# Output by pairs of token blocks on the upper and lower 64 lanes, and combine weights split on ScalarE and VectorE

## The chip, the core and the metric

One Trainium2 chip, one of its cores. The metric is the device time of one execution of the program, in microseconds (us). Before the change three runs took 404.69, 405.67 and 407.14 us, a median of 405.67. Engines are named as the profile names them: PE (TensorE matmul) and PEld (its weight loads), DVE (VectorE), ACT (ScalarE), POOL (GpSimd), SP (SyncE, which issues every DMA here).

## What is computed

Decayed causal attention over 8 batches, 8 heads and 576 tokens, whose output, as x of 4608 tokens by 512 columns, goes through a soft mixture of 8 experts with 4 slots each (32 slots):

```python
scores = where(causal, -1e9, q @ k.T / 8 + cum[:, None] - cum[None, :])
x = softmax(scores) @ v                      # 4608 tokens x 512
logits = x @ phi                             # 4608 x 32
d = softmax(logits, over tokens)             # dispatch
slot_out[e] = relu((d.T @ x)[e] @ w1[e]) @ w2[e]
c = softmax(logits, over slots)              # combine weights
out = c @ slot_out                           # 4608 x 512
```

All inputs and the output are float32. The last product, c times slot_out, is what the change is about: 4608 tokens by 32 slots by 512 columns, and 9.44 MB to be written to memory.

## The kernel before

The order of all instructions of an engine is the order in which the code writes them; nothing is rescheduled. Attention runs as a pipeline over 32 pairs of heads (the loop over `g`, from line 681). Meanwhile 23 of the 64 weight tiles of the experts (512 KB each, called quarters, 128 lanes by 1024 floats) are loaded into `w` tiles that stay in place; another 18 go into buffers that attention gives up at its end (`wstream`, line 124), and the last 23 are loaded into the first 23 tiles again, each as soon as the matmuls that read the old quarter are done. All these loads stand in SP's queue, in the order in which the experts use them.

After attention comes a tail. Slot inputs are summed up (`dispatch`, line 444), normalised, and then `STEPS` (line 35) lists, expert by expert, when its first matmul (`mlp1`, line 867) and the two halves of its second (`mlp2`, line 899) stand in PE's order. Experts 4 to 7 have their second matmul cut by output columns: the left 256 columns (half 0) come first, in the loop; the right 256 (half 1) come in the code behind the loop, whose eight weight quarters are the last eight to arrive.

Combine weights: `ctok` holds c by tokens. `split(b)` (line 655) takes batches b and b+4 and writes a rounded copy `hi` and the remainder `lo` to `cw`, both on POOL; `cols` (line 662) turns them on PE and copies them to `cT` on ACT. So `cT` has 128 lanes: lanes 0 to 63 are hi and lo of the 32 slots of batches 0 to 3, lanes 64 to 127 those of batches 4 to 7, and its 2304 columns are 18 blocks of 128 tokens. `split(0)` and `split(1)` stand at the last pair of heads (line 789), `split(2)` in the tail (836), `split(3)` at line 937, and `cols(3)` on line 939, behind the second matmul of expert 0.

Output: `gathered(n)` (line 965) adds half n of the columns of slot_out up in `so`, `slots(n)` (969) copies it to all lanes by a matmul, and `halve(h, n)` (972) splits it into a rounded part and a remainder, for the lower 64 lanes (h = 0) or the upper (h = 1); the other 64 lanes of these four `SO` tiles were filled with zeros on POOL (952). `blocks(n0, n1, c)` (981) makes token blocks n0 to n1 of 36: two matmuls of all 128 rows each, rounded part and remainder, into one PSUM bank, a copy to a stage tile (ACT and DVE in turn), and one DMA for the group. There are four banks for this and six stage tiles of 1024 columns. A block of one column half is 128 KB in rows of 1 KB; a whole one is 256 KB in rows of 2 KB. The first 20 blocks (`FIRST`) are made by halves, and the left halves of 15 of them stand between the last `mlp2` matmuls, three blocks to each weight quarter from the second of expert 5 on; the other 16 are made whole.

Of the kernel before, what the change touches and what calls it, by code (L numbers as in the profile page):

```python
# [16 lines left out]
NE, SPE, DM, DF = 8, 4, 512, 1024  # L17
NS = NE * SPE
P = 128
NPAIR = H // 2  # L20
NG = B * NPAIR
NBLK = 5
# [7 lines left out]
NQ = 8 * NE  # L30
QW = 1024
DEFER = 4
FIRST = 20

STEPS = (
    (0, 0), (1, 0), (2, 0), (3, 0), (0, 4), (0, 6), (1, 4), (1, 6), (4, 0), (5, 0), (2, 4), (2, 6), (3, 4), (3, 6),
# [34 lines left out]
def attn_softmoe(ctx: ExitStack, tc: tile.TileContext, qk, v, f, phi, w1, w2, cst, out):  # L71
# [89 lines left out]
    def turn():  # L161
        ring.append(ring.pop(0))
        return ring[-1]
# [488 lines left out]

    CW = {}

    def split(b):

        CW[b] = tp.tile([P, NBLK, 2, 2, NS], F32R, name=f"cw{b}", tag="cw", bufs=2)
        hi, lo = (CW[b][:, :, :, r].rearrange("p t h s -> p h t s") for r in range(2))
        nc.gpsimd.tensor_copy(hi, ctok[:, b::4])
        nc.gpsimd.tensor_tensor(lo, ctok[:, b::4], hi.bitcast(F32), op=ALU.subtract)  # L660

    def cols(b, bank):

# [17 lines left out]
    for g in range(1, NG):  # L681
# [104 lines left out]
        norm(h0)  # L786
        if g == 31:
            wstream(PTS[:, 0:QW])
            split(0)
            split(1)  # L790
        s3(h1)
        if w == 0:
            logits(b, *range(NPAIR))
# [10 lines left out]
    b = B - 1  # L804
    ring += [ps_s.tile([P, 512], F32, name=f"more{n}", tag="s") for n in range(2)]
    norm(NH - 1)
    dispatch(b - 1, 0, 1, 2)
    xt(NG - 1, (0, 4), nc.scalar.copy)
    xt(NG - 1, (2, 3), nc.vector.tensor_copy)
# [23 lines left out]
    nc.vector.tensor_reduce(mb[:, 2:3], EX[:, 0:192], axis=AX.X, op=ALU.add)  # L833
    total(b)
    nc.vector.tensor_scalar_mul(fin[:, 0:2], ones, lrun)
    split(2)
    dispatch(b, *range(NBLK))
    wstream(X[2], X[3])
    next(c2)
# [79 lines left out]
    for e, k in STEPS[:-4]:  # L919
        if k == 0:  # L920
            mlp1(e, 0, 1, 2, 3)
            relu(e)
        else:
            mlp2(e, k // 2 - 2)
        n = used + (2 if k else 4)
        wstream(*quarter[used : min(n, NRES)])
        used = n
        if (e, k) in ((2, 0), (4, 0), (6, 0), (5, 4)):
            own({2: 0, 4: 2, 6: 4, 5: 6}[e])
        if (e, k) == (1, 0):  # L930
            weigh(b)
            tokens(b, 0)
            combine(b, 0)
        if (e, k) == (3, 0):
            combine(b, 1)
            combine(b, 2)
            split(3)
        if (e, k) == (0, 6):
            for _ in cols(3, turn):
                pass  # L940
        if (e, k) == (1, 6):
            blank_h(4)
            blank_h(5)
        if (e, k) == (5, 0):
            late.close()
            sp = ctx.enter_context(tc.tile_pool(name="sp", bufs=1))
            so = sp.tile([P, DM], F32, name="so")

            SO = [[sp.tile([P, DM], F32R, name=f"SO{h}{r}") for r in range(2)] for h in range(2)]
            for h in range(2):  # L950
                for r in range(2):
                    nc.gpsimd.memset(SO[h][r][64 * (1 - h) : 64 * (1 - h) + 64].bitcast(F32), 0.0)
        if (e, k) == (3, 6):
            nc.scalar.copy(so, pv[0])
            blank_h(6)
            blank_h(7)

    half = [slice(256 * n, 256 * n + 256) for n in range(2)]
    pr = [t[:, 0:256] for t in bank]
    outv = out.rearrange("(n p) c -> p n c", p=P)  # L960
    NT = B * S // P
    stage = [t.rearrange("p a b -> p (a b)") for t in RAW] + p2 + p0
    copies = [nc.scalar.copy, nc.vector.tensor_copy]

# [4 lines left out]
    def slots(n):  # L969
        nc.tensor.matmul(pr[n], srep, so[:, half[n]], start=True, stop=True)  # L970

    def halve(h, *ns):
        rows = slice(64 * h, 64 * h + 64)
        for n in ns:
            c = half[n]
            nc.scalar.copy(SO[h][0][rows, c], pr[n][rows])
            nc.vector.tensor_tensor(SO[h][1][rows, c], pr[n][rows], SO[h][0][rows, c].bitcast(F32), op=ALU.subtract)

    state = [0, 0, 0]

    def blocks(n0, n1, c=slice(0, DM)):

        w = c.stop - c.start
        if state[1] + w * (n1 - n0) > QW:
            state[0:2] = state[0] + 1, 0
        o = stage[state[0] % len(stage)][:, state[1] : state[1] + w * (n1 - n0)]
        state[1] += w * (n1 - n0)
        for n in range(n0, n1):
            h, m = divmod(n, NT // 2)
            pm = turn()[:, 0:w]  # L990
            for r in range(2):
                nc.tensor.matmul(pm, cT[:, 128 * m : 128 * m + 128], SO[h][r][:, c], start=(r == 0), stop=(r == 1))  # L992
            copies[state[2] % 2](o[:, w * (n - n0) : w * (n - n0 + 1)], pm)
            state[2] += 1
        nc.sync.dma_start(outv[:, n0:n1, c], o.rearrange("p (n c) -> p n c", c=w))

    gathered(0)
    mlp2(4, 1, 0)
    slots(0)
    mlp2(4, 1, 1)  # L1000
    halve(0, 0)
    mlp2(5, 1, 0)
    n = 0
    for e, k in ((5, 1), (6, 0), (6, 1), (7, 0), (7, 1)):
        blocks(n, n + 2, half[0])
        mlp2(e, 1, k)
        blocks(n + 2, n + 3, half[0])
        n += 3
        if n == 9:
            halve(1, 0)  # L1010
    gathered(1)
    blocks(n, n + 2, half[0])
    slots(1)
    blocks(n + 2, n + 3, half[0])
    halve(0, 1)
    blocks(n + 3, FIRST, half[0])
    for n in range(0, FIRST, 2):
        blocks(n, n + 2, half[1])
        if n == 4:
            halve(1, 1)  # L1020
    for n in range(FIRST, NT, 2):
        blocks(n, n + 2)


# [39 lines left out]
```

## Time and profile before

| | |
|---|---|
| median of three runs | 405.67 us |
| the profiled execution: its own time | 407.26 us |
| the span of that profile | 405.5 us |
| PE busy in the span | 385.3 us (95%) |
| DVE, ACT, POOL busy | 281.7, 259.2, 257.6 us |
| attention's last matmuls with values end at | 331.8 us |
| last weight load is issued at | 366.6 us |
| first output DMA is issued at | 374.83 us |
| bytes moved by DMA | 93.72 MB |

The page cuts the span into 40 slices of some 10 us, with a digit for each engine's busy share; below them stand the clock granted to TensorE, the busy share of the 16 DMA engines and the GB/s that they moved. A row of windows gives for one stretch the busy time of each engine, with the number of instructions, then the granted clock, the DMA share and GB/s. The chain of waits is the work that ended last, followed back from the end: start, length, engine, tile, line. A group row gives a line's instructions of one shape: count, busy time and mean of one in ns, and behind the second bar the idle time before them. PE's single matmul records overlap one another, so what a matmul costs in a row of them is read from the chain, not from their mean.

### The profile page before, as it was taken

To read this page: it belongs to the slowest core of one execution; us is meant where nothing else is said; L and a number is where in the kernel's file an instruction comes from. 1 tells how busy PE (TensorE), PEld (TensorE's weight loads), DVE (VectorE), ACT (ScalarE), POOL (GpSimd) and SP (SyncE) were. 2 spreads that over 40 slices of the span, in tenths; PEclk is the share of its full clock that TensorE was granted. 3 is DMA by queue.
4 is the path that set the end of the run, shared out by engine and by line. 5 is a ranking of instruction groups with operands and counts; after the bars stand their busy time and mean duration, and the time that the engine had idled before them with its cause. 6 is when DMAs were issued, how large, how long until landed. Compare 5 with 4: busy or idle time off the path is not lost.

```text
span 405.5 us, 15191 instructions
## 1 busy us (share of the span) xinstructions
PE 385.3 (95%) x5871; PEld 339.3 (84%) x5871; DVE 281.7 (69%) x1127; ACT 259.2 (64%) x660; POOL 257.6 (64%) x351
## 2 busy tenths in 40 slices
PE   7888999999999999999999999999999999899990
PEld 6678999999999999998999999999999885345780
DVE  7784787878787977796879787878787533312571
ACT  8847776767786777686767786778685443100561
POOL 4694788777777777787778777877787742120000
PEclk9996999999999999999999999999999999999997
DMA  6773566677867787768767767777765699999698
GB/s 207 183 183 108 150 174 181 204 205 210 254 192 221 207 238 211 203 191 254 200 197 210 221 205 206 205 207 206 203 172 152 227 360 375 381 408 391 239 368 335
DMA packets 35192, 93.72 MB, mean 231 GB/s; under 512 B 4282, under 2 KB 10096, under 8 KB 35120
## 3 DMA queue, kind: packets, MB, share of 16 engines
q1 hardware_dynamic: 35120, 92.75, 74.0%
q8 instruction: 46, 0.75, 0.8%
q14 instruction: 26, 0.21, 0.1%
HBM read 63.93 MB, written 9.73 MB: 182 GB/s over the span
## 4 chain that ended last, share of the span: by engine, by line
PE 81%; DMA 4%; DVE 3%; ACT 3%; issue 1%; POOL 0%; SPq 0%; DVEq 0%; ACTq 0%
PE pv L309 24%; PE ring L274 13%; PE ring L275 11%; PE s L224 11%; PE pv L336 4%; DMA RAW<-in_qk 3%; PE lg L372 2%; PE pv L911 2%; PE ds L453 2%; PE ring L874 2%; PE pv L874 2%; PE more L992 2%; DVE s L237 1%; DMA out<-RAW 1%; PE ring L911 1%; PE ring L992 1%
## 5 line engine op out<-in xcount | busy, mean ns | idle before, releaser
L281 ACT ACTIVATE PTS<-ring 128x320 f32<-128x320 f32 (+2 forms) x256 | 119.7, 513 | 64.3 <-PE ring L275 36.7
L237 DVE CUSTOM_DVE_ANT_0 s<-s,mask 128x320 f32<-128x320 f32 (+4 forms) x320 | 137.7, 449 | 10.4 <-PE s L224 5.9
L274 PE MATMUL ring<-YA,WA 67*128 67x320 f32 (+9 forms) x384 | 123.3, 334 | 2.7 <-ACT PTS L281 1.7
L275 PE MATMUL ring<-YB,WB 128*128 128x320 f32 (+4 forms) x384 | 111.7, 299 | 0.0
L309 PE MATMUL pv<-V,PTS 128*64 128x65 f32 x3200 | 105.0, 224 | 0.6 <-ACT mr L256 0.6
L309 PEld LDWEIGHTS pv<-V,PTS 128*64 128x64 f32 x3200 | 100.3, 138 | 3.2 <-issue 1.2
L224 PE MATMUL s<-WA,YA 66*128 66x288 f32 (+9 forms) x384 | 98.9, 314 | 1.6 <-ACT YA L182 0.8
L203 POOL TENSOR_TENSOR WB<-RAW,WB 64x576 fp32r<-64x576 f32 x64 | 90.3, 1411 | 11.7 <-DMA WB<-WA 4.9
L208 POOL TENSOR_TENSOR YB<-RAW,YA 64x576 fp32r<-64x576 f32 x64 | 89.3, 1413 | 2.4
L274 PEld LDWEIGHTS ring<-YA,WA 67*128 67x128 f32 (+3 forms) x384 | 70.6, 185 | 9.0 <-issue 2.1
L275 PEld LDWEIGHTS ring<-YB,WB 128*128 128x128 f32 (+1 forms) x384 | 70.8, 184 | 0.0
L224 PEld LDWEIGHTS s<-WA,YA 66*128 66x128 f32 (+1 forms) x384 | 63.6, 192 | 7.3 <-ACT YA L182 1.1
L289 POOL TENSOR_SCALAR_AFFINE_SELECT PTS<-PTS 128x384 f32<-128x384 f32 x64 | 33.3, 521 | 32.0 <-ACT PTS L281 27.8
L292 POOL TENSOR_SCALAR_AFFINE_SELECT PTS<-PTS 128x128 f32<-128x128 f32 (+1 forms) x128 | 31.3, 265 | 34.8 <-ACT PTS L281 32.1
L237 DVE DVE_READ_ACCUMULATOR2_ANT MT<- 128x1 f32 x372 | 52.7, 142 | 0.0
L177 ACT CAST WA<-RAW 64x576 fp32r<-64x576 f32 x64 | 40.0, 669 | 14.2 <-DMA RAW<-in_qk 13.2
L336 PE MATMUL pv<-cs,X 128*128 128x128 f32 x155 | 42.9, 278 | 1.0 <-DVE X L329 0.8
L182 ACT CAST YA<-RAW 64x576 fp32r<-64x576 f32 x64 | 40.0, 670 | 0.4
L237 DVE CUSTOM_DVE_ANT_0 s<-s,mask,MT 128x288 f32<-128x288 f32 x62 | 32.6, 526 | 9.8 <-PE s L224 0.9
L324 DVE TENSOR_SCALAR rl<-pv 128x5 f32<-128x5 f32 x64 | 10.5, 164 | 34.7 <-PE pv L309 33.8
L329 DVE TENSOR_TENSOR X<-pv,rl 128x320 f32<-128x320 f32 (+1 forms) x65 | 31.5, 486 | 2.4 <-DMA YA<-mr 0.3
L360 ACT COPY XT<-pv 128x128 f32<-128x128 f32 (+1 forms) x124 | 28.7, 292 | 0.0
(202 smaller groups left out, 355.1 us busy)
## 6 DMA issues: line engine op xcount, KB each, us to landing
w<-in_w SPq DMA_DIRECT2D x46, 512.0 KB
RAW<-in_qk SPq DMA_DIRECT2D x31, 576.0 KB
V<-in_v SPq DMA_DIRECT2D x32, 325.0 KB
WB<-WA SPq DMA_DIRECT2D x31, 288.0 KB
YB<-YA SPq DMA_DIRECT2D x31, 288.0 KB
p<-in_w SPq DMA_DIRECT2D x7, 512.0 KB
out<-RAW SPq DMA_DIRECT2D x5, 512.0 KB
out<-RAW SPq DMA_DIRECT2D x9, 256.0 KB
```

Of the source, the lines that this page charges most:

```text
L177: nc.scalar.copy(WA[g % 3][0:64, S * h : S * h + S], RAW[g % 3][64:128, h])
L182: nc.scalar.copy(YA[g % 3][0:64, h, 64:640], RAW[g % 3][0:64, h])
L203: nc.gpsimd.tensor_tensor(t[0:64], RAW[g % 3][64:128, h], t[64:128].bitcast(F32), op=ALU.subtract)
L208: nc.gpsimd.tensor_tensor(YB[g % 2][64:128, h], RAW[g % 3][0:64, h], YA[g % 3][0:64, h, 64:640].bitcast(F32), op=ALU.subtract)
L224: nc.tensor.matmul(t[:, o : o + w], ya[0:m, h, 128 * blk : 128 * blk + 128], wa[0:m, j0 : j0 + w], start=True, stop=True)
L237: nc.vector.tensor_tensor_reduce(out=t[:, o : o + w], in0=t[:, o : o + w], in1=mask[:, m0 : m0 + w], scale=1.0, scalar=top if n == 3 else ...
L274: nc.tensor.matmul(o, wa[0:m, j0 : j0 + n], ya[0:m, h, 64 + i0 : 64 + i0 + w], start=True, stop=False)
L275: nc.tensor.matmul(o, wb[:, j0 : j0 + n], yb[:, h, i0 : i0 + w], start=False, stop=True)
L281: nc.scalar.activation(PT[i % 2][:, SEG_O[bank] : SEG_O[bank] + at], t[:, 0:at], AF.Exp, scale=0.125)
L289: nc.gpsimd.affine_select(d3, d3, pattern=[[0, 3], [1, 128]], compare_op=ALU.is_ge, fill=0.0, base=0, channel_multiplier=-1)
L309: nc.tensor.matmul(o[64 * u : 64 * u + 64, t, :], PT[i % 2][:, at : at + 64], V[:, g % 2, c, 65 * h : 65 * h + 65], start=(c == 0), stop=( ...
L336: nc.tensor.transpose(pm[:, 0:128], x[:, t, 128 * (p % 2) : 128 * (p % 2) + 128], ident)
```

## The change

- `split` makes `hi` on ACT and `lo` on DVE; nothing of it is left on POOL. For batches 0 and 1, `hi` stands where the whole split stood and `lo` behind the last normalisation of attention, on DVE.
- `cols(3)` moves two steps on, behind the second matmul of expert 1.
- `SO` is two tiles of 128 full lanes (rounded part, remainder), without zeros; `halve(n)` fills all lanes at once. The four memsets on POOL go.
- `blocks` goes by pairs: for m of 18, block m (batches 0 to 3) on lanes 0 to 63 and block m + 18 (batches 4 to 7) on lanes 64 to 127: four matmuls of 64 rows, the lower and the upper in turn, into two banks. ACT copies the lower block, DVE the upper. A single pair goes out in one DMA, two pairs in one DMA for each side.
- `FIRST` is 8 pairs, so 16 blocks are made by halves and 20 whole. No pair stands between the matmuls of one expert any more: two pairs behind expert 5, two behind expert 6, the rest behind expert 7.
- PSUM banks: two more for the output behind expert 5, two more behind the second `halve`.

```diff
-FIRST = 20
+FIRST = 8
...
-    def split(b):
+    def split(b, *parts):
...
-        nc.gpsimd.tensor_copy(hi, ctok[:, b::4])
-        nc.gpsimd.tensor_tensor(lo, ctok[:, b::4], hi.bitcast(F32), op=ALU.subtract)
+        if 0 in parts:
+            nc.scalar.copy(hi, ctok[:, b::4])
+        if 1 in parts:
+            nc.vector.tensor_tensor(lo, ctok[:, b::4], hi.bitcast(F32), op=ALU.subtract)
...
-            split(0)
-            split(1)
+            split(0, 0)
+            split(1, 0)
...
     norm(NH - 1)
+    split(0, 1)
+    split(1, 1)
...
-        if (e, k) == (0, 6):
+        if (e, k) == (1, 6):
             for _ in cols(3, turn):
...
+    def halve(n):
+        nc.scalar.copy(SO[0][:, half[n]], pr[n])
+        nc.vector.tensor_tensor(SO[1][:, half[n]], pr[n], SO[0][:, half[n]].bitcast(F32), op=ALU.subtract)
...
+    def blocks(m0, m1, c=slice(0, DM)):
...
+        for m in range(m0, m1):
+            pm = [turn()[:, 0:w] for _ in range(2)]
             for r in range(2):
-                nc.tensor.matmul(pm, cT[:, 128 * m : 128 * m + 128], SO[h][r][:, c], start=(r == 0), stop=(r == 1))
+                for h in range(2):
+                    rows = slice(64 * h, 64 * h + 64)
+                    nc.tensor.matmul(pm[h], cT[rows, 128 * m : 128 * m + 128], SO[r][rows, c], start=(r == 0), stop=(r == 1))
+            for h in range(2):
+                copies[h](o[:, h, m - m0], pm[h])
...
-    mlp2(5, 1, 0)
-    n = 0
-    for e, k in ((5, 1), (6, 0), (6, 1), (7, 0), (7, 1)):
-        blocks(n, n + 2, half[0])
-        mlp2(e, 1, k)
-        blocks(n + 2, n + 3, half[0])
-        n += 3
-        if n == 9:
-            halve(1, 0)
+    halve(0)
+    mlp2(5, 1)
+    ring += [bank[0], po[0]]
+    blocks(0, 1, half[0])
+    blocks(1, 2, half[0])
+    mlp2(6, 1)
+    blocks(2, 3, half[0])
+    blocks(3, 4, half[0])
+    mlp2(7, 1)
     gathered(1)
+    blocks(4, 6, half[0])
     slots(1)
+    blocks(6, FIRST, half[0])
+    halve(1)
+    ring += [bank[1], po[1]]
+    for m in range(0, FIRST, 2):
+        blocks(m, m + 2, half[1])
+    for m in range(FIRST, NT // 2):
+        blocks(m, m + 1)
```

Where PE turns the combine weights of batches 3 and 7 (lines 668 and 671, tiles `lg` and `ring` from `cw`): before, it comes between the first two experts' second matmuls (line 911, into `pv`).

```order
L911 MATMUL pv_148<-w_135,X_99 32x512 x2
L668 MATMUL lg_5604<-cs,cw_5905 128x128 x2
L668 MATMUL ring_150<-cs,cw_5905 128x128 x2
L668 MATMUL ring_150<-cs,cw_5905 128x64
L911 MATMUL pv_148<-w_136,X_100 32x512 x2
```

After, on PE at the same place, the second matmul of expert 1 (line 916) comes first.

```order
L916 MATMUL pv_148<-w_136,X_100 32x512 x2
L916 MATMUL pv_148<-w_137,X_100 32x512 x2
L916 MATMUL pv_148<-w_138,X_100 32x512 x2
L916 MATMUL pv_148<-RAW_97,X_100 32x512 x2
L671 MATMUL lg_5604<-cs,cw_5905 128x128 x2
```

So four rows of 512-column matmuls now stand ahead of the turning.

Where PE begins the output, before: the two weight quarters of expert 5 in half 1 (`w_133` and `w_134`, line 911) with the first two blocks between them (line 992).

```order
L911 MATMUL pv_148<-w_133,X_100 32x256 x4
L992 MATMUL ring_150<-SO_5984,cT 128x256
L992 MATMUL ring_150<-SO_5985,cT 128x256
L992 MATMUL more_5686<-SO_5984,cT 128x256
L992 MATMUL more_5686<-SO_5985,cT 128x256
L911 MATMUL pv_148<-w_134,X_100 32x256 x4
```

After, on PE at the same place (line 993 is the output matmul, 916 the expert's):

```order
L916 MATMUL pv_148<-w_133,X_100 32x256 x4
L916 MATMUL pv_148<-w_134,X_100 32x256 x4
L993 MATMUL ring_150<-SO_5984,cT 128x256
L993 MATMUL more_5684<-SO_5984,cT 128x256
L993 MATMUL ring_150<-SO_5985,cT 128x256
L993 MATMUL more_5684<-SO_5985,cT 128x256
```

Two quarters now stand together, and the two banks of a pair take turns.

Where DVE ends attention, after: the two remainders of `split` (line 663) have come in between the last normalisation (329) and the copy of turned tokens (345).

```order
L329 TENSOR_TENSOR X_5475<-pv_149,rl_5686 128x2x64
L329 TENSOR_TENSOR X_5475<-pv_149,rl_5686 128x3x64
L663 TENSOR_TENSOR cw_5640<-ctok,cw_5640 128x2x5x32
L663 TENSOR_TENSOR cw_5642<-ctok,cw_5642 128x2x5x32
L345 COPY XT_105<-ring_150 128x256
```

Before, the rows of lines 329 and 345 stood next to each other, and four instructions on POOL did the work.

More of the change, by code (lines that the diff above doesn't have):

```diff
@@ L653, in attn_softmoe @@
     CW = {}
-    def split(b):
-        CW[b] = tp.tile([P, NBLK, 2, 2, NS], F32R, name=f"cw{b}", tag="cw", bufs=2)
+    def split(b, *parts):
+        if 0 in parts:
+            CW[b] = tp.tile([P, NBLK, 2, 2, NS], F32R, name=f"cw{b}", tag="cw", bufs=2)
         hi, lo = (CW[b][:, :, :, r].rearrange("p t h s -> p h t s") for r in range(2))
-        nc.gpsimd.tensor_copy(hi, ctok[:, b::4])
-        nc.gpsimd.tensor_tensor(lo, ctok[:, b::4], hi.bitcast(F32), op=ALU.subtract)
+        if 0 in parts:
+            nc.scalar.copy(hi, ctok[:, b::4])
+        if 1 in parts:
+            nc.vector.tensor_tensor(lo, ctok[:, b::4], hi.bitcast(F32), op=ALU.subtract)
     def cols(b, bank):
@@ L835, in attn_softmoe @@
     nc.vector.tensor_scalar_mul(fin[:, 0:2], ones, lrun)
-    split(2)
+    split(2, 0, 1)
     dispatch(b, *range(NBLK))
@@ L936, in attn_softmoe @@
             combine(b, 2)
-            split(3)
-        if (e, k) == (0, 6):
+            split(3, 0, 1)
+        if (e, k) == (1, 6):
             for _ in cols(3, turn):
@@ L947, in attn_softmoe @@
             so = sp.tile([P, DM], F32, name="so")
[L949 to L952, printed above, removed]
+            SO = [sp.tile([P, DM], F32R, name=f"SO{r}") for r in range(2)]
         if (e, k) == (3, 6):
@@ L959, in attn_softmoe @@
     pr = [t[:, 0:256] for t in bank]
-    outv = out.rearrange("(n p) c -> p n c", p=P)
     NT = B * S // P
+    outv = out.rearrange("(h m p) c -> p h m c", h=2, p=P)
     stage = [t.rearrange("p a b -> p (a b)") for t in RAW] + p2 + p0
@@ L970, in slots @@
         nc.tensor.matmul(pr[n], srep, so[:, half[n]], start=True, stop=True)
[L972 to L977, printed above, removed]
+    def halve(n):
+        nc.scalar.copy(SO[0][:, half[n]], pr[n])
+        nc.vector.tensor_tensor(SO[1][:, half[n]], pr[n], SO[0][:, half[n]].bitcast(F32), op=ALU.subtract)
     state = [0, 0, 0]
-    def blocks(n0, n1, c=slice(0, DM)):
+    def blocks(m0, m1, c=slice(0, DM)):
         w = c.stop - c.start
-        if state[1] + w * (n1 - n0) > QW:
+        n = 2 * w * (m1 - m0)
+        if state[1] + n > QW:
             state[0:2] = state[0] + 1, 0
[L986 to L990, printed above, removed]
-            for r in range(2):
[L992 to L995, printed above, removed]
+        o = stage[state[0] % len(stage)][:, state[1] : state[1] + n].rearrange("p (h m c) -> p h m c", h=2, c=w)
+        state[1] += n
+        for m in range(m0, m1):
+            pm = [turn()[:, 0:w] for _ in range(2)]
+            for r in range(2):
+                for h in range(2):
[3 more added lines that the diff above has]
+                copies[h](o[:, h, m - m0], pm[h])
+        if m1 - m0 == 1:
+            nc.sync.dma_start(outv[:, :, m0, c], o[:, :, 0])
+        else:
+            for h in range(2):
+                nc.sync.dma_start(outv[:, h, m0:m1, c], o[:, h])
     gathered(0)
@@ L1000, in attn_softmoe @@
     mlp2(4, 1, 1)
-    halve(0, 0)
-    mlp2(5, 1, 0)
-    n = 0
-    for e, k in ((5, 1), (6, 0), (6, 1), (7, 0), (7, 1)):
-        blocks(n, n + 2, half[0])
-        mlp2(e, 1, k)
-        blocks(n + 2, n + 3, half[0])
-        n += 3
-        if n == 9:
-            halve(1, 0)
+    halve(0)
[7 more added lines that the diff above has]
+    mlp2(7, 1)
     gathered(1)
-    blocks(n, n + 2, half[0])
+    blocks(4, 6, half[0])
     slots(1)
[L1014 to L1022, printed above, removed]
+    blocks(6, FIRST, half[0])
[5 more added lines that the diff above has]
+        blocks(m, m + 1)
 def kernel(q, k, v, f, moe_phi, moe_w1, moe_w2):
```

## The prediction

> **What bounds the kernel now.** I read the page's slices first, then windows over the tail, then the chain of waits there. In the page the last two rows are the busy share of the DMA engines and their GB/s, a slice each of some 10 us.
>
> ```profile
> DMA  6773566677867787768767767777765699999698
> GB/s 207 183 183 108 150 174 181 204 205 210 254 192 221 207 238 211 203 191 254 200 197 210 221 205 206 205 207 206 203 172 152 227 360 375 381 408 391 239 368 335
> ```
>
> Up to slice 31 the DMA engines have room. From slice 33 they are full (9), with one hole, the 6 and 239 GB/s near 375 to 385 us. The windows place it; the last column is GB/s, the one before it the DMA share.
>
> ```profile
> 341.20:347.00 5.80, 5.80 (x100) 3.23 (x99) 2.09 (x7) 0.87 (x4) 0.00 (x0) 1.00 0.93 315
> 347.00:374.00 27.00, 25.09 (x339) 11.82 (x339) 5.61 (x20) 2.04 (x6) 4.41 (x10) 1.00 1.02 407
> 374.00:384.00 10.00, 9.70 (x86) 6.65 (x85) 5.42 (x14) 4.60 (x13) 0.00 (x0) 1.00 0.64 224
> 384.00:390.00 6.00, 5.98 (x41) 5.31 (x40) 4.56 (x12) 4.21 (x11) 0.00 (x0) 1.00 1.03 348
> 390.00:393.00 3.00, 3.00 (x15) 2.40 (x14) 2.22 (x4) 1.76 (x3) 0.00 (x0) 1.00 1.09 382
> 393.00:404.00 11.00, 3.32 (x15) 2.34 (x13) 3.15 (x5) 2.35 (x4) 0.00 (x0) 0.88 1.04 397
> 403.00:404.00 1.00, 0.00 (x0) 0.00 (x0) 0.00 (x0) 0.00 (x0) 0.00 (x0) 0.50 0.92 342
> ```
>
> From 347 to 374 weights stream at 407 GB/s, a quarter (0.524 MB) each 1.29 us. From 384 to 404 output streams with full DMA engines: column halves (1 KB rows) at 348 to 382, whole blocks (2 KB rows) at 397. Bytes end at about 403.9, by the 342 of the last microsecond. So the tail is bound by DMA on both sides of the hole. At the 348 of the stretch behind it, the hole is worth 10 x (1 - 224/348) = 3.6 us, all that an earlier output can win. What makes it is in the chain, whose PE rows I take as the prices of PE work.
>
> ```profile
> 343.19 1.73 PE ring L874 x32
> ...
> 351.08 0.46 POOL cw L659
> 351.54 0.07 issue
> 351.61 0.87 POOL cw L660
> 352.48 0.04 issue
> 352.52 0.44 PE lg L668 x2
> 352.96 0.42 PE ring L668 x3
> 353.38 1.85 PE pv L911 x16
> ...
> 371.60 0.70 PE pv L970 x2
> 372.30 1.00 PE pv L911 x16
> 373.30 0.43 PE ring L992 x2
> 373.73 0.23 PE more L992 x2
> 373.96 0.57 PE pv L911 x8
> ...
> 380.18 0.57 PE pv L911 x8
> ```
>
> Expert matmuls run without a pause from 372.3 to 380.75, and three output blocks stand between each two of their weight quarters: two blocks 0.43 and 0.23 us, eight expert matmuls 0.57. The left half of the output trickles, and the right half can only begin behind 380.75. The hole is a matter of PE's order.
>
> **The change, part by part.** *The turning of the last combine weights.* PE waits for POOL's split here (in the bracket the idle time before, and for whom):
>
> ```profile
> 352.52 0.44 PE L668 MATMUL lg<-cs,cw 128*128 128x128 f32 x2 [1.36 <-POOL cw L660]
> ```
>
> So PE was through with the matmuls before it at 351.16. After the change the next 16 (1.85 us in the chain) come first and last until 353.0; hi and lo on ACT and DVE, 0.5 each (below), begin at 351.08 like POOL's and are done at 352.1: the wait goes. DMA is full here (407), so nothing arrives sooner; PE alone comes 1.36 us earlier to 372.3.
>
> *The other splits.* The prices, by groups (the first number behind the bar is busy us, the second the mean in ns):
>
> ```profile
> L660 POOL TENSOR_TENSOR cw<-ctok,cw 128x320 fp32r<-128x320 f32 x4 | 3.5, 868 | 0.3
> L329 DVE TENSOR_TENSOR X<-pv,rl 128x320 f32<-128x320 f32 x3 | 1.5, 492 | 0.3 <-DMA YA<-mr 0.3
> L993 ACT COPY RAW<-ring 128x256 f32<-128x256 f32 x6 | 2.2, 374 | 2.8 <-PE ring L992 2.7
> L993 DVE COPY RAW<-more 128x256 f32<-128x256 f32 x5 | 2.1, 423 | 2.2 <-PE more L992 2.0
> L992 PEld LDWEIGHTS more<-SO,cT 128*128 128x128 f32 x56 | 8.6, 188 | 2.5 <-issue 0.8 <-DVE RAW L993 0.4 <-DVE p L993 0.3
> ```
>
> No row shows lo on DVE. Its bounds are 0.49 (the same size, one operand in PSUM) and POOL's 0.87; I take 0.49, since it is the same engine. On DVE two of them stand between these rows, and one ahead of the last:
>
> ```profile
> 332.27 0.56 DVE L329 TENSOR_TENSOR X<-pv,rl 128x128 f32<-128x128 f32 x2
> 334.20 0.42 DVE L345 COPY XT<-ring 128x256 f32<-128x256 f32 x1 [1.37 <-PE ring L336]
> 339.03 0.23 DVE L835 TENSOR_SCALAR fin<-cs,lrun 128x2 f32<-128x2 f32 x1
> 339.86 0.35 DVE L459 SCALAR_TENSOR_TENSOR acc<-acc,mb,ring 128x128 f32<-128x128 f32 x1 [0.60 <-PE ring L453]
> ```
>
> and on ACT the three hi, 0.47 each by 0.374 for 256 columns, two ahead of the first row and one ahead of the second:
>
> ```profile
> 333.98 0.32 ACT L345 COPY XT<-ring 128x192 f32<-128x192 f32 x1 [4.43 <-PE ring L336]
> 340.17 0.37 ACT L673 CAST cT<-ring 128x256 fp32r<-128x256 f32 x1 [1.85 <-PE ring L668]
> ```
>
> Two take 0.98 of DVE's 1.37 us of waiting for PE, the one 0.49 of 0.60. Cost nothing; at 0.87 each they would put 0.4 and 0.3 us on the path, 0.7 together. Behind the waiting DVE stand the copy of turned tokens, which PE's last logits need, and `acc`. ACT's waits of 4.43 and 1.85 us hold the hi. The memsets on POOL lay beside 407 GB/s of weights and PE rows that did not wait for them; they give nothing. SP issues 26 output DMAs in place of 31, all behind the last weight load as before.
>
> *The start of the output.* The first output DMA, and the microseconds around it:
>
> ```profile
> 374.00 0.43 DVE L993 COPY RAW<-more 128x256 f32<-128x256 f32 x1 [0.85 <-PE more L992]
> 374.83 1.49 SPq L995 DMA_DIRECT2D out<-RAW  x3
> ...
> 374.00:375.00 1.00, 1.00 (x12) 0.59 (x12) 0.43 (x1) 0.14 (x2) 0.00 (x0) 1.00 0.70 279
> 375.00:376.00 1.00, 1.00 (x13) 0.46 (x11) 0.42 (x1) 0.74 (x2) 0.00 (x0) 1.00 0.44 164
> 376.00:377.00 1.00, 1.00 (x10) 0.85 (x14) 0.49 (x2) 0.30 (x1) 0.00 (x0) 1.00 1.02 340
> ```
>
> A DMA is issued 0.40 us behind the copy and runs fully 1.2 us behind its issue (376.0). The weights fade at 279 and 164: the slowest DMA engines finish the last quarter between 375 and 377. I take 376.5, and 375.2 and 373.9 for the two before it. No row of before shows PE waiting for them, since it uses them later, the last at 380.18.
>
> *Row tiles.* A pair is four matmuls of 64 rows. One after another they cost 0.46 at 256 columns (two of 128 rows: 0.23); side by side, 0.23. The nearest row is four column tiles of 32: 32 matmuls of 256 columns in 1.73 us, 0.054 each against 0.115, so two run at once. I take 0.23. A pair's two copies run side by side in 0.42, a DMA of 256 KB takes 0.262/348 = 0.75: copies do not bound. Against this stands the Trainium skill, "TensorE: Matmul & The Clock Gate", The mechanism: a weight load overlaps a running matmul only in another row group. Here two 128-row matmuls took 0.23 with a load of 0.188 to each, in the same row group, so the trace disagrees; by the rule each second pair of matmuls would wait for its loads.
>
> *The chain after the change.* PE comes to the expert matmuls at 370.94, does 24 in 1.50 (16 took 1.00), two pairs in 0.66 (0.20 for the change of work, as 0.43 against 0.23) until 373.1; the first pair is through PE at 372.9 and copied at 373.4 (0.1 to begin, 0.42), its DMA issued at 373.8 and at full rate from 375.0 instead of 376.0. Expert 6 ends behind its second quarter at 374.4, two more pairs at 375.1, expert 7 behind the last quarter at 377.0. Eight half blocks (1.05 MB, 3.0 us at 348) and the weights' rest (some 0.2 MB, 0.5 us) keep the DMA busy until 378.5. Then `gathered(1)` on DVE until 377.5 (0.42, as a copy of that size), the two copies of pairs 4 and 5 until 378.4, issue 378.8, bytes 380.0: **a hole of 1.5 us stays**, since these pairs stand behind the last weights. Pairs 6 and 7 follow in time, copied at 379.4, and keep the DMA busy until 383.0. `halve(1)` (0.37 and 0.42) ends at 380.2, two pairs on PE at 380.7, their copies at 381.6, and they run from 383.2: 0.2 more. Then 16 half blocks (2.10 MB) at 359, the mean of 348 and 382 over their 9 us: 5.8; ten whole pairs (5.24 MB) at 397: 13.2. Bytes end at 402.2 instead of 403.9: **1.7 us less**. In it are 0.3 us for 1.05 MB that go in wide rows now (2.9 at 359, 2.6 at 397).
>
> The profiled execution took 407.26, 1.59 above the median of 405.67: it would become 405.6, the median **404.0 us**.
>
> **The rivals.** *The weights are no obstacle.* Should the last quarter be there by 375.2, expert 7 ends 1.3 us sooner, the hole all but closes, and the gain is 3.0: 402.7. For it: 407 GB/s and quarters of 1.29 us; against it: the fading 279 and 164.
>
> *The hole only moves.* If loads or tiles go one after another, a pair costs up to 2 x (0.115 + 0.188) = 0.61 in place of 0.23. Ahead of the last weights that hides; behind them pairs 4 and 5 come 0.76 later and the first right halves another 0.76. The gain shrinks to 0.2: 405.5. For it: no row shows row tiles; against it, the loads hidden in before. The rule on loads that the Trainium skill gives under The mechanism would lead here too. Lo on the path at 0.87 would end near here too. That the pairs are not made as the change says is no rival: the order of PE shows them.
>
> *Slower: PE paces the output.* If all four matmuls and their loads follow one another, a pair costs 4 x (0.115 + 0.188) = 1.21, a whole one 4 x (0.235 + 0.188) = 1.69. It decides from 1.31 on, what the DMA needs for 512 KB at 400. From 381.5 on PE would need 8 x 1.21 + 10 x 1.69 = 26.6, until 408.1, and the last copy and DMA 3.5 more, an estimate (0.6 + 0.4 + 1.2 + 1.3): bytes end at 411.6, 7.7 us later, for a time of 413. Only hidden loads and the overlap of column tiles in before speak against it.
>
> **How the numbers follow.** A measurement of this kernel can tell about 0.5% from no change, 2.0 us: faster is below 403.6, slower above 407.7. The forecast, 404.0 with its own range of 403.0 to 405.0, has a chance of 0.50; about a third of it lies below 403.6. The weights being no obstacle has 0.18, the hole that only moves 0.26, PE pacing 0.06. Faster: 0.18 + 0.16 = 0.34; slower: 0.06 and 0.01 for the splits on top of a hole that moves, 0.07; the same: 0.59. The range runs from 402.2, half a microsecond beyond the first rival, to 406.0, beyond the second; the third and some scatter of runs (before: 404.69 to 407.14) are left out.
>
> **What would show it.** In the profile after: no wait of PE at the turning, and expert 4's first right-half matmuls 1.4 us earlier; PE waiting for a weight DMA ahead of expert 7's last matmuls; first output DMA near 373.8; one hole of 1 to 2 us near 378.5 and full DMA from 383; a pair of 256-column blocks in 0.23 us. I am wrong if expert 7 does not wait, if a pair costs 0.46 or more, or if PE's row ahead of the copies fills the time from 383 on.

## The result, and the profile after

The kernel after took 404.38 us (median of 18 runs, 400.85 to 408.3); the kernel before, timed beside it, 406.67 (18 runs, 403.45 to 410.59). The ratio is 0.9924, with a 95% interval of 0.9897 to 0.9951: faster by 3.1 us, by 2.0 to 4.2. All ratios here leave out the slow runs, those more than 1.5% above the fastest of the same kernel, so they are not the quotients of the medians, which stand 2.3 us apart. The profiled execution of after took 403.23 us, its span is 401.5.

First the two spans have to be made comparable. Attention's last matmuls with values, in after and then in before (start, length):

```profile
326.27 3.25 PE L309 MATMUL pv<-V,PTS 128*64 128x65 f32 x100
```

```profile
328.56 3.25 PE L309 MATMUL pv<-V,PTS 128*64 128x65 f32 x100
```

They end at 329.52 and 331.81. So of the 4.0 us between the spans 2.29 are there before the first instruction that the change touches has any effect (`hi` on ACT, at 327.18 in after); where they come from is shown near the end. What the change can be judged by is the part from here to the span's end, called the **tail** from now on: 73.69 us in before, 71.98 in after, 1.71 less. Times of after are put on before's clock by adding 2.29.

The page of after, its last two rows of slices:

```profile
DMA  6756666677867777778777777777765789999798
GB/s 206 184 134 170 180 174 195 210 205 210 244 191 219 211 217 211 207 198 249 200 202 208 224 207 207 208 208 207 206 160 152 244 310 392 366 409 406 277 386 342
```

There is a hole still, the 7 and 277 GB/s of slice 38. The windows place it (the last column is GB/s):

```profile
374.50:379.50 5.00, 3.67 (x38) 2.40 (x40) 2.60 (x7) 1.84 (x7) 0.00 (x0) 1.00 0.60 206
379.50:387.70 8.20, 7.56 (x61) 5.37 (x57) 5.94 (x14) 5.36 (x14) 0.00 (x0) 1.00 1.07 374
371.70:381.70 10.00, 7.86 (x93) 5.32 (x91) 5.65 (x17) 4.56 (x16) 0.00 (x0) 1.00 0.78 276
381.70:391.70 10.00, 6.78 (x37) 3.79 (x33) 5.80 (x10) 4.64 (x9) 0.00 (x0) 0.82 1.06 386
```

The last two rows begin 42.18 and 52.18 us behind attention's end, as 374 and 384 us do in before. The first of them moves 276 GB/s where before moved 224, 520 KB more; the second 386, where the same stretch of before has

```profile
383.99:393.99 10.00, 9.98 (x58) 8.53 (x57) 7.53 (x16) 6.55 (x15) 0.00 (x0) 1.00 1.06 365
```

another 210 KB. At 386 GB/s that is 1.35 and 0.54 us, together about what the tail lost. The hole, 3.6 us deep before, has not closed. What holds it open is first PE's order, now with waits for weights (start, length, in the bracket the wait):

```profile
367.87 0.70 PE L972 MATMUL pv<-so,cs 128*128 128x256 f32 x2 [0.17 <-DVE so L969]
368.50 1.07 PE L916 MATMUL pv<-w,X 128*32 128x256 f32 x16
369.90 0.64 PE L916 MATMUL pv<-w,X 128*32 128x256 f32 x8 [0.33 <-DMA w<-in_w]
...
372.45 0.64 PE L916 MATMUL pv<-w,X 128*32 128x256 f32 x8 [0.64 <-DMA w<-in_w]
...
374.97 0.64 PE L916 MATMUL pv<-w,X 128*32 128x256 f32 x8 [0.64 <-DMA w<-in_w]
375.54 0.38 PE L993 MATMUL more<-SO,cT 64*128 64x256 f32 x1
375.55 0.38 PE L993 MATMUL lg<-SO,cT 64*128 64x256 f32 x1
```

The second quarters of experts 5, 6 and 7 are waited for. Four of the eight half pairs were made by 374.97; the other four, and everything in the right half, follow that last wait. SP's output DMAs tell the same (start of the first of a group; x4 is four pairs, and the x2 below are the two sides of pairs 4 and 5):

```profile
371.87 3.10 SPq L997 DMA_DIRECT2D out<-RAW  x4
376.75 1.85 SPq L1000 DMA_DIRECT2D out<-RAW  x2
```

### The profile page after: what moved, and what is told of

It reads as the page before. It is cut to its first block, busy times and chain, and to the rows that moved or that the text cites. A ratio compares the mean times of both kernels' runs of the same rounds, so it can differ in the third digit from the quotient of the medians.

```text
span 401.5 us, 15138 instructions
## 1 busy us (share of the span) xinstructions
PE 378.8 (94%) x5863; PEld 332.2 (83%) x5863; DVE 281.3 (70%) x1127; ACT 258.5 (64%) x660; POOL 251.1 (63%) x339
## 4 chain that ended last, share of the span: by engine, by line
PE 84%; DMA 6%; DVE 2%; ACT 1%; issue 0%; SPq 0%; ACTq 0%; DVEq 0%
PE pv L309 25%; PE ring L274 14%; PE ring L275 12%; PE s L224 12%; PE pv L336 4%; PE lg L372 3%; DMA w<-in_w 3%; PE pv L916 2%; PE ds L453 2%; PE ring L879 2%; PE pv L879 2%; DMA out<-p 1%; DMA YA<-mr 1%; PE pv L247 1%; PE tk L436 1%; DMA out<-RAW 1%
## 5 line engine op out<-in xcount | busy, mean ns | idle before, releaser
L237 DVE CUSTOM_DVE_ANT_0 s<-s,mask,MT 128x288 f32<-128x288 f32 x62 | 32.6, 526 | 10.2 <-PE s L224 1.2
```

Source lines behind the costliest of these rows:

```text
L237: nc.vector.tensor_tensor_reduce(out=t[:, o : o + w], in0=t[:, o : o + w], in1=mask[:, m0 : m0 + w], scale=1.0, scalar=top if n == 3 else ...
```

## The experiments

Theory: the tail is shorter because PE loses no time at the turning of the combine weights and pairs go side by side; what is left of the hole is the last weight quarters, which PE waits for. Rivals: row tiles side by side bring nothing; only one of the two parts of the change brings all; PE, not the weights, paces the tail. All runs at a glance, in order; the fifth column is the GB/s of the 10 us that begin 42.18 us behind attention's end:

| kernel | attention ends | span | tail | GB/s there | ratio to before (95%) |
|---|---|---|---|---|---|
| before | 331.81 | 405.5 | 73.69 | 224 | |
| after | 329.52 | 401.5 | 71.98 | 276 | 0.9924 (0.9897 to 0.9951) |
| 1 all rows | 333.74 | 406.2 | 72.46 | 232 | 0.9996 (0.9959 to 1.0032) |
| 2 splits alone | 333.43 | 405.6 | 72.17 | 275 | 1.0008 (0.9975 to 1.0041) |
| 3 output alone | 330.20 | 402.5 | 72.30 | 247 | 0.9985 (0.9952 to 1.0018) |
| 4 no last wait | 329.72 | 400.7 | 70.98 | 298 | 0.9943 (0.9904 to 0.9983) |
| 5 pairs ahead | 327.95 | 398.1 | 70.15 | 360 | 0.9924 (0.9883 to 0.9966) |
| 6 after again | 332.52 | 404.1 | 71.58 | 269 | 0.9969 (0.9935 to 1.0003) |
| 7 after, PE kept warm | 348.08 | 419.1 | 71.02 | | 1.0325 (1.0273 to 1.0376) |
| 8 before, PE kept warm | 344.37 | 417.2 | 72.83 | | 1.0378 (1.0327 to 1.0429) |
| 9 pairs ahead, all rows | 333.15 | 404.9 | 71.75 | 284 | 0.9953 (0.9911 to 0.9995) |
| 10 before again | 328.45 | 402.4 | 73.95 | 222 | 1.0013 (0.9973 to 1.0053) |
| 11 pairs ahead again | 331.17 | 401.3 | 70.13 | 343 | 0.9918 (0.9883 to 0.9954) |

Spans of the same kernel differ by some 3 us, with attention's end. Their tails agree within 0.4 us: 73.69 and 73.95, 71.98 and 71.58, 70.15 and 70.13. Kernels 7 and 8, whose tails run the code of after and before, lie 0.6 to 1.1 us below those. So a tail from a single profile is good to some 0.4 us at best, and a difference of less than 1 us between two of them says little by itself.

**1, all rows.** After, but every output matmul over all 128 rows, so that no two lie side by side; each output block then holds the sum of a lower and an upper one.

```diff
-                    rows = slice(64 * h, 64 * h + 64)
-                    nc.tensor.matmul(pm[h], cT[rows, 128 * m : 128 * m + 128], SO[r][rows, c], start=(r == 0), stop=(r == 1))
+                    nc.tensor.matmul(pm[h], cT[:, 128 * m : 128 * m + 128], SO[r][:, c], start=(r == 0), stop=(r == 1))
```

> The changed kernel, but each output matmul reads all 128 rows, so no two run side by side (each block then sums both lane halves; its values are not the reference's). Every other instruction, copy and DMA stays. The tail is the time from the end of attention's last value matmuls on PE to the end of the span: 73.7 us in the profile before (331.8 to 405.5), 72.0 in the profile after (329.5 to 401.5). Theory: the last weights pace the end of the experts and the DMA paces the rest, so PE's time for a pair (0.23 becoming 0.46) shows only behind the last weights, in the pairs of the hole: the tail becomes 72.3 to 73.0, 0.3 to 1.0 longer than after, and still shorter than before. Rival, the row tiles are the gain: the tail goes back to 73.7 or more, and the time with it to that of the kernel before.

Measured: a tail of 72.46, 0.5 and 0.9 us more than after's two, and a ratio that shows no gain (0.9996). The tail agrees with the theory, the whole time with the rival's second half; its interval still holds the 0.997 that the tail would give. In the chain of waits (start, length), four of after's matmuls first:

```profile
375.93 0.11 PE more L993
376.04 0.00 PE lg L993
376.04 0.12 PE pv L993
376.16 0.00 PE ring L993
```

and here:

```profile
380.35 0.12 PE more L992
380.47 0.12 PE lg L992
380.59 0.12 PE pv L992
380.71 0.11 PE ring L992
```

In after every second step costs nothing: two row tiles take the time of one, and a pair 0.23 us. Without them a pair takes 0.46. So the row tiles run side by side, and in this order they are worth less than a microsecond.

**2, splits alone.** Before, with `hi` on ACT, `lo` on DVE and the turning behind expert 1's second matmul; output as before.

```diff
...
-        nc.gpsimd.tensor_copy(hi, ctok[:, b::4])
-        nc.gpsimd.tensor_tensor(lo, ctok[:, b::4], hi.bitcast(F32), op=ALU.subtract)
+        if 0 in parts:
+            nc.scalar.copy(hi, ctok[:, b::4])
+        if 1 in parts:
+            nc.vector.tensor_tensor(lo, ctok[:, b::4], hi.bitcast(F32), op=ALU.subtract)
...
-        if (e, k) == (0, 6):
+        if (e, k) == (1, 6):
```

> The kernel before with only the splits on ScalarE and VectorE and the turning of the last combine weights moved behind expert 1. Theory: PE comes 1.36 us earlier to the last experts, the first output DMA goes out 1.0 to 1.4 us earlier against the tail's start, and the woven order keeps its hole: the tail shortens by 0.8 to 1.3, from 73.7 to 72.4 to 72.9. Rival 1, the whole gain is here: 72.0 or less. Rival 2, the weights pace PE anyway and nothing is gained: 73.5 or more.

Measured: a tail of 72.17, 1.5 us less than the first tail of before and a little better than expected. The first output DMA is issued here:

```profile
375.02 3.84 SPq L1000 DMA_DIRECT2D out<-RAW  x6
```

That is 41.59 us behind attention's end, where before has 43.02: all of the turning's wait arrives at the output. The ratio, 1.0008, doesn't show it, and its interval leaves out the 0.996 that the tail would give. One profile's tail and twelve runs disagree here; which of them is off stays open. In that profile attention took some 0.5 us longer than in the others (284.8 us, see the start below), which would be a third of the gain.

**3, output alone.** After, with both split operations on POOL again and the turning at its old place.

```diff
-            nc.scalar.copy(hi, ctok[:, b::4])
+            nc.gpsimd.tensor_copy(hi, ctok[:, b::4])
...
-            nc.vector.tensor_tensor(lo, ctok[:, b::4], hi.bitcast(F32), op=ALU.subtract)
+            nc.gpsimd.tensor_tensor(lo, ctok[:, b::4], hi.bitcast(F32), op=ALU.subtract)
...
-        if (e, k) == (1, 6):
+        if (e, k) == (0, 6):
             for _ in cols(3, turn):
```

> The changed kernel with the splits back on GpSimd and the turning back behind the first expert, so the wait of 1.36 us is there again. Theory: expert 7's last matmuls wait for the last weights in the changed kernel (0.64 us at each of three quarters), so most of the 1.36 us is swallowed there; what stands behind the last weights sets the end: the tail is within 0.5 us of that of the changed kernel, 72.0 to 72.5. Rival, the two parts add up: 73.0 or more, the changed kernel's tail with the 1.36 us on top.

Measured: a tail of 72.30. Its table of waits (in total, times, longest; us):

```profile
PE lg L671 <- POOL cw L663: 1.4, 1, 1.4
PE pv L914 <- DMA w<-in_w: 0.6, 1, 0.6
```

and that of after:

```profile
PE pv L916 <- DMA w<-in_w: 1.6, 3, 0.6
```

Part of the 1.4 us that PE loses at the turning comes back as less waiting for weights. So each part alone takes some 1.5 us from the tail, and both together 1.7 to 2.0: the parts do not add. In the new order the reason shows: of the turning's 1.4 us, 0.6 to 1.0 is waited for the last weights instead (1.6 us in after, as 0.33, 0.64 and 0.64, and 1.2 in kernel 6, for 0.6 here). That one part is the sole source falls, since each brings about as much without the other. By how much both beat the better part, 0.2 to 0.6 us, is within the scatter of the tails, and the whole times of kernels 2 and 3 set neither apart from before.

**4, no last wait.** After, but expert 7's right half reads the last quarter of expert 5, which is there long before; the output is not the sum over the right weights.

```diff
-    def mlp2(e, half, *ks):
+    def mlp2(e, half, *ks, src=None):
...
-            w = weights(e, 4 + 2 * half + k)
+            w = weights(src[0] if src else e, 4 + 2 * half + (src[1] if src else k))
...
-    mlp2(7, 1)
+    mlp2(7, 1, 0, src=(5, 1))
+    mlp2(7, 1, 1, src=(5, 1))
```

> The changed kernel, but expert 7's right half reads the last quarter of expert 5 in place of its own two (its values are not the reference's), so that PE doesn't wait for the last two loads, which are still made. Theory: the hole that stays in the DMA's work is the wait for the last weights; without it expert 7 ends about 1.3 us earlier and the tail shortens by 1.0 to 1.5, to 70.5 to 71.0. Rival, the hole comes from the chain behind expert 7 (sum, slots, halve, copies, DMA start) or from DMA itself: the tail shortens by less than 0.5, to 71.5 or more.

Measured: a tail of 70.98, 1.0 and 0.6 us less than after's. The last quarter's lateness is on the path, as the theory has it: the output DMA of pairs 4 and 5 is issued 46.54 us behind attention's end, 0.7 earlier than after's 47.23. But it is not the whole hole: 298 GB/s, for some 385 when it is full. The waits for the second quarters of experts 5 and 6 are still there, and the tail holds a second difference, a shorter stop of SP (see The hole below), so the 0.6 to 1.0 is not the wait's alone.

**5, pairs ahead.** What follows from 3 and 4: PE should have output to make while it waits. Ten half pairs in place of eight, nine of them ahead of the last five weight quarters.

```diff
-FIRST = 8
+FIRST = 10
...
-    mlp2(5, 1)
     ring += [bank[0], po[0]]
-    blocks(0, 1, half[0])
-    blocks(1, 2, half[0])
-    mlp2(6, 1)
-    blocks(2, 3, half[0])
-    blocks(3, 4, half[0])
-    mlp2(7, 1)
+    mlp2(5, 1, 0)
+    m = 0
+    for e, k, n in ((5, 1, 1), (6, 0, 2), (6, 1, 2), (7, 0, 2), (7, 1, 2)):
+        for _ in range(n):
+            blocks(m, m + 1, half[0])
+            m += 1
+        mlp2(e, 1, k)
     gathered(1)
-    blocks(4, 6, half[0])
+    blocks(m, FIRST, half[0])
     slots(1)
-    blocks(6, FIRST, half[0])
     halve(1)
```

> The changed kernel with ten pairs by halves in place of eight, of which nine stand ahead of the last weight quarter of expert 7 (one, two, two, two and two between the quarters, in the times in which PE waits for the loads) and the tenth right behind it. Theory: the hole that stays in the changed kernel is a lack of finished pairs while PE waits for the last weights and makes the right half ready; nine pairs (2.36 MB, 6 us of DMA) fill it, and the tail shortens by 1.5 to 2.5, from 72.0 to 69.5 to 70.5. Rival, the start of the output only trades with the weights' arrival (more output on the DMA engines delays the last quarters, and the right half with them): the tail stays within 0.5 of 72.0.

Measured: 404.4 us beside 405.99 of before, a ratio of 0.9924; a tail of 70.15. The 10 us of the hole and PE in the middle of it:

```profile
370.13:380.13 10.00, 9.36 (x107) 6.57 (x105) 7.15 (x20) 6.11 (x20) 0.00 (x0) 1.00 1.02 360
```

```profile
372.18 0.64 PE L916 MATMUL pv<-w,X 128*32 128x256 f32 x8
372.74 0.38 PE L993 MATMUL more<-SO,cT 64*128 64x256 f32 x1
...
373.41 0.64 PE L916 MATMUL pv<-w,X 128*32 128x256 f32 x8
```

The DMA share is 1.02 where after has 0.78, and no matmul waits for a weight. Expert 7's last quarter is begun 45.46 us behind attention's end, as in after (45.45): the pairs fit into time that PE had waited, and the earlier output does not hold the weights up beyond it. The hole is filled, as forecast.

**6, after again, and 10, before again.** No edit; second samples of both.

> The changed kernel as it is, beside the others. Theory: 1.7 us of the 3.1 us between the medians are the change, the rest is chance: in the profiles so far attention ends anywhere between 329.5 and 333.7 us, by whether the half clock at the start falls at 20 or at 32 us and lasts 6.8 or 10.2 us; so the tail is 71.7 to 72.4 again and the ratio to the kernel before lies near 0.996, between 0.992 and 1.000. Rival, the change gains in attention too: ratio at 0.9925 or less once more.

> The kernel before, as a second sample of itself. Theory 1 (the whole time of a run scatters with the stretch of half clock at its start, the part behind attention's end does not): ratio 0.9965 to 1.0035, the part behind attention's end 72.8 to 73.8 us (73.69 and 72.83 in the two profiles so far), whatever the span. Theory 2 (the part behind attention's end scatters as much as the gain): below 72.5.

Measured: after again 405.42 us, ratio 0.9969, tail 71.58; before again 408.11 us, ratio 1.0013, tail 73.95, a little above what was expected. The mean tails, 73.82 and 71.78, are 2.0 us apart. That is inside both intervals of after's ratio, and at the edge of the first.

**7 and 8, PE kept warm.** After and before, with plain float32 matmuls whose results nobody reads put where PE waits near 18, 28 and 30 us.

```diff
+    def keep(n):
+        for _ in range(n):
+            nc.tensor.matmul(pv[1][:, 453:512], cs[:, 0:128], cs[:, 0:59], start=True, stop=True)
...
+    warm(10, cs)
...
+        if g == 1:
+            keep(24)
         px(g - 1, 0)
...
+        if g == 1:
+            keep(44)
```

> The changed kernel with idle matmuls (results not used) on PE at three places near 18, 28 and 30 us where it waits for ScalarE and VectorE. Theory: the clock of TensorE is halved after such a pause, wherever it finds one; with the pauses filled there is no stretch at half clock near 20 or 32 us, attention ends at 328.5 us or sooner in every run, and the times scatter by less than 2 us instead of 7. Rival, the half clock has another cause: it comes as before, attention ends between 329.5 and 334, and the matmuls that were added only cost time.

> The kernel before with the same idle matmuls at the start. Theory: the same as for the changed kernel with them; then the difference of the two in whole time is that of their tails, 1.4 to 2.0 us. Rival, the change gains outside the tail: 3 us between the two.

Measured: ratios to before of 1.0325 and 1.0378. What was expected of the start did not come: attention ends at 348.08 and 344.37 us, and the six runs of each kernel spread over some 20 us. The matmuls were far dearer than I thought; in 8 the group of `keep(24)` is

```profile
32.30 5.57 PE L495 MATMUL pv<-cs 128*128 128x59 f32 x48 [0.77 <-DVE X L329]
```

The 24 matmuls are 48 instructions in the profile, so one of 59 columns cost 2 x 0.116 = 0.23 us. With that the whole time says nothing; the tails, 71.02 and 72.83, are 1.8 us apart, which agrees with the other pairs. On the clock see below.

**9, pairs ahead, all rows.** Kernel 5 with the edit of 1, and the sums mixed in the same way.

> The order of the faster version (nine pairs ahead of the last weight quarters, the tenth behind), but every output matmul runs over all 128 rows, so no two row tiles lie side by side; the sums of a lower and an upper block are mixed by that, and only the time is read. A half pair costs PE 0.46 us in place of 0.23. Theory 1 (PE has room ahead of the last weights, since the order left it waiting for them until now): of the nine pairs' 2.1 us at most 0.5 shows, span behind attention's end 70.2 to 70.9 us against 70.15. Theory 2 (with the weights no longer waited for, PE paces expert 7's end and each pair counts): expert 7's end and the tail 1.5 to 2.1 us later, 71.6 to 72.3.

Measured: a tail of 71.75, 1.6 us above kernel 5. The last weight quarter's matmuls begin here in 9, and in 11 below:

```profile
380.63 0.64 PE L916 MATMUL pv<-w,X 128*32 128x256 f32 x8
```

```profile
376.54 0.64 PE L916 MATMUL pv<-w,X 128*32 128x256 f32 x8
```

47.48 and 45.37 us behind attention's end: 2.1 us, nine times 0.23. The second theory holds: with the weights out of the way PE paces the left half, and each pair counts. In the 10 us that begin 52.18 us behind attention's end PE has no pause in 9, and the DMA falls to 360 GB/s, where kernel 11 has 382:

```profile
385.33:395.33 10.00, 10.00 (x57) 8.47 (x55) 7.55 (x15) 6.51 (x14) 0.00 (x0) 1.00 1.02 360
```

```profile
383.35:393.35 10.00, 4.50 (x25) 2.31 (x21) 5.42 (x8) 4.20 (x8) 0.00 (x0) 0.80 1.06 382
```

**11, pairs ahead again.** No edit to 5.

> The version with nine pairs ahead of the last weight quarters, as a second sample. Theory 1 (the hole in the output's DMA is filled for good): the part behind attention's end 69.7 to 70.7 us, ratio to the kernel before 0.990 to 0.996. Theory 2 (its 0.9924 and 70.15 us were chance of one profile): above 71.3 us, ratio above 0.997.

Measured: 404.3 us, ratio 0.9918, tail 70.13. Kernel 5 beats before by about 0.8% in both samples, by 3.7 us in the tail. Against after its tail is 1.6 us shorter; in whole times the two were not set apart (0.9883 to 0.9966 against 0.9935 to 1.0003, beside the same runs of before).

## Why the prediction was right or wrong

It was right in the mechanism and, for the tail, in the size: 1.7 us forecast, 1.71 in the first pair of profiles, 2.0 between the means of two. The median forecast, 404.0, was measured at 404.38; that this fits so closely is luck, since before, timed beside it, stood at 406.67 and not at the 405.67 from which the 1.7 us were taken. By its steps:

- **The turning: right.** PE no longer waits there:

```profile
349.98 0.60 PE L916 MATMUL pv<-RAW,X 128*32 128x512 f32 x2
350.51 0.44 PE L671 MATMUL lg<-cs,cw 128*128 128x128 f32 x2
```

  The first matmuls behind `slots(0)`, at 368.50, are 370.79 on before's clock, 1.5 us ahead of the 372.30 of before; 1.4 were expected.
- **The splits: right.** Groups (busy us, mean in ns):

```profile
L663 DVE TENSOR_TENSOR cw<-ctok,cw 128x320 fp32r<-128x320 f32 x4 | 1.9, 486 | 0.5 <-ACT cw L661 0.5
L661 ACT CAST cw<-ctok 128x320 fp32r<-128x320 f32 x4 | 1.8, 463 | 4.6 <-DVE ctok L484 4.6
```

  0.49 for lo, taken from the subtraction of the same size on DVE, is what it took, and 0.46 for hi against 0.47. In kernel 2 the output starts earlier by the whole of POOL's wait, so nothing of it reaches the path.
- **Row tiles: right.** 0.23 for a pair, the two tiles starting 0.00 to 0.01 us apart in the rows above, 3 to 4 ns in the trace. The Trainium skill, "TensorE: Matmul & The Clock Gate", Why this matters for your kernels, says that tiles in distinct row groups run at once, starting within 4 ns: the trace agrees. The Trainium skill's rule under The mechanism of that page, which the prediction weighed, that a weight load overlaps a running matmul only in another row group, is contradicted again: matmuls over all 128 rows follow one another at 0.12 us in kernels 1 and 9, with a load of 0.19 us to each.
- **The last weights: 0.8 us off in one sample, 0.2 in the other.** I took 373.9, 375.2 and 376.5 for the last three quarters. PE's waits end at 372.45 and 374.97, on before's clock 374.7 and 377.3, for the first and third of them; expert 5's second quarter, at 372.2, was waited for too, which I had not seen. So the first output DMA came at 374.2 and not 373.8, and expert 7 ended at 377.8 and not 377.0. In kernel 6, the same code, the waits end here:

```profile
374.83 0.64 PE L916 MATMUL pv<-w,X 128*32 128x256 f32 x8 [0.58 <-DMA w<-in_w]
377.36 0.64 PE L916 MATMUL pv<-w,X 128*32 128x256 f32 x8 [0.64 <-DMA w<-in_w]
```

  That is 42.31 and 44.84 us behind attention's end, for the 42.09 and 44.69 that I took; expert 5's second quarter is not waited for, and the first output DMA, at 41.83, is 0.2 ahead of the forecast. So the step was right, and what it left out is that the last weights move by some 0.6 us from one execution to the next. The fading 279 and 164 GB/s in the profile of before had shown only that the last quarter ends somewhere in 2 us.
- **The rate of half blocks: mis-sized the other way.** I took 359 GB/s, a mean of before's rows; behind the hole they ran at 374. The 24 half blocks behind it (3.15 MB) take 8.4 us at that rate where the prediction had 3.0 and 5.8, and its second gap of 0.2 us, ahead of the right halves, did not come. These two, 0.4 and 0.2 us, cancel most of the 0.8 of the late weights in the first profile; that the sum fits so well there is luck. In kernel 6, with the weights in time, the tail came out 0.4 us shorter than the forecast's 72.0.
- **The hole: right in kind, with a cause left out.** Behind the last weights the DMA runs at 206 GB/s for 5 us: at 374 that is 2.2 us, for the 1.5 and 0.2 forecast. DMA is full from 379.5, 381.8 on before's clock. The list of signs says 383, but the chain has the output running from 380.0 on: by that it came 1.8 us late, and the late weights are 0.8 of it. Pairs 6 and 7 did not "follow in time". SP issued the second DMA of pairs 4 and 5 here (the three times are shortest, median and longest, in ns), and the DMA stopped a second time:

```profile
L1000 SPq DMA_DIRECT2D out<-RAW x1: 1390/1390/1390, 377.2 to 377.2; - x1
...
377.50:378.50 1.00, 0.22 (x4) 0.15 (x2) 0.83 (x3) 0.80 (x3) 0.00 (x0) 1.00 0.70 249
378.50:379.50 1.00, 0.92 (x12) 0.72 (x14) 0.49 (x2) 0.27 (x2) 0.00 (x0) 1.00 0.39 130
```

  The issue just ahead of it took 0.37 us. Between 377.24 and 378.19 a transfer of 16 KB lands on the queue that the page calls instruction, and the issue ends 0.4 us behind it. The same meeting is in ten more of the profiles, with issues of 1.46 to 2.31 us that end 0.3 to 0.4 behind such a transfer; before has 2.04 us at 380.70, its second sample 2.31. Kernel 4's is 0.86, and kernel 7, where the transfer came 3 us sooner and held up no issue, has a tail 0.6 to 1.0 us shorter than after's two. So part of the hole is SP's and not PE's. Of the gain it can be only a part: before's stop is 0.6 to 0.8 us longer than after's, but kernel 2, with 1.93 us, has its 1.5 us of gain all the same. The prediction has no term for it, and what it costs was not tried.
- **The rivals.** That the weights are no obstacle falls with the three waits and with kernel 4. That the hole only moves falls with the pair at 0.23 us. That PE paces the output holds, for the left half, only in kernel 9, where pairs cost double and nothing else is in the way.

What the sum did not hold is the rest of the first comparison: 3.1 us there, 1.3 in kernel 6, 2.0 in the tail. In the two profiles the rest is the start, where both kernels run the same code. The third hundred of the matmuls with values, before and then after:

```profile
47.48 3.25 PE L309 MATMUL pv<-V,PTS 128*64 128x65 f32 x100
45.37 3.25 PE L309 MATMUL pv<-V,PTS 128*64 128x65 f32 x100
```

2.11 of the 2.29 us are there by then. From the start of this hundred to attention's end it takes 284.3 and 284.1 us in before's two profiles, 284.2 and 284.0 in after's, and 283.8 to 284.8 in the other seven without added matmuls, while the hundred itself starts anywhere between 44.1 and 49.8. So the change gains nothing worth naming in attention. That the 18 runs of each kernel differ by 3.1 us for the same reason fits, but they have no profiles to show it. The clock is the column ahead of the DMA share; before, then after:

```profile
26.00:32.00 6.00, 3.55 (x42) 2.95 (x41) 4.68 (x20) 3.20 (x7) 4.00 (x3) 1.00 0.92 264
32.00:40.00 8.00, 8.00 (x75) 7.54 (x76) 4.06 (x16) 5.07 (x15) 4.11 (x8) 0.57 0.18 57
```

```profile
14.00:20.00 6.00, 4.86 (x33) 4.28 (x32) 4.84 (x20) 5.41 (x11) 3.13 (x8) 0.96 0.79 221
20.00:26.00 6.00, 6.00 (x63) 5.64 (x63) 3.16 (x14) 3.38 (x8) 5.32 (x7) 0.50 0.59 138
```

TensorE's clock is halved for a stretch of 6.8 us in both, near 20 us in one execution and near 32 in the other, and attention ends 2.29 us apart. Place and length go with attention's end whatever the kernel: with the stretch near 20 it ends at 327.95 and 328.45 (3.4 us long; kernels 5 and 10), 329.52 and 329.72 (6.8; after, 4) and 330.20 (10.2; 3), with the stretch near 32 at 331.81 and 331.17 (6.8; before, 11) and between 332.52 and 333.74 (10.2; 6, 9, 2, 1).

## What to carry to other kernels

When a stage is bound by what lands last, read for each edit what waits next: two edits worth 1.5 us each alone gave 1.7 to 2.0 together, because much of the time that one of them won was waited for the last weights. Give the waiting engine work that needs none of what it waits for (kernel 5), and only then does making that work cheaper pay: the row tiles were worth 0.5 to 0.9 us in the old order and 1.6 in the new one, by one profile without them in each. When an output stage is made of many small DMAs, look at each issue as well: one that takes 1.4 us in place of 0.4 doesn't show among the groups of a page. And where runs scatter with something at the start, compare profiles from the last point at which both kernels have done the same.

## What the hardware showed that I had not expected

- **Half clock at the start.** In twelve of the thirteen profiles the clock shows one stretch of 3.4, 6.8 or 10.2 us between 19 and 43 us. With the matmuls of kernel 8 there was none (1.00 in both rows), with those of kernel 7 there was one:

```profile
5.00:50.00 45.00, 40.87 (x380) 38.12 (x379) 22.07 (x82) 21.08 (x42) 16.85 (x20) 1.00 0.48 131
50.00:400.00 350.00, 346.64 (x5600) 306.27 (x5599) 249.22 (x1023) 228.71 (x604) 236.78 (x323) 1.00 0.75 231
```

```profile
24.00:32.00 8.00, 7.85 (x88) 7.03 (x87) 3.76 (x18) 3.34 (x9) 7.73 (x9) 0.50 0.50 139
```

  The Trainium skill, "TensorE: Matmul & The Clock Gate", What's actually happening, has the clock halved after an idle window of about 3.4 us, and windows that run free of the kernel. The lengths agree with windows of that size. But PE is busy for 3.55 of the 6 us ahead of the stretch in before and for 4.86 of 6 in after, so no such window was idle throughout. That pauses bring the stretch about is what kernel 8 speaks for and kernel 7 against; the cause was not settled.
- **Rows of 1 KB went faster than before's profile had shown:** 374 GB/s over 8.2 us in after, beside 348 over 6 us in before. What makes the difference was not tried.
- **Plain float32 matmuls are dear.** Each is two instructions in the profile. In kernel 8 one of 59 columns took 0.23 us, where one of 256 columns with rounded inputs takes 0.115 in the output: almost nine times as much by the column. The three plain matmuls of 192 columns that before has at its start (line 489) are six instructions that begin 0.16 us apart, so 0.33 us each, 3.8 times by the column:

```profile
13.07 1.14 PE L489 MATMUL ring<-cs 128*128 128x192 f32 x6
```

  The Trainium skill, "FP8 and Floating Point Precision", TensorE Precision Notes, has four passes through the array for true float32. At 192 columns that agrees; at 59, four passes would be 0.11 us by the rounded price, an estimate, and the trace has twice that. What is paid on top was not tried, and the row that could have warned me stood in before's profile.
